# Attention and a gated feed-forward layer on one core: separate places for the inputs of the first four jobs, and mean durations in the planner

## The chip, the cores and the metric

The kernel runs on one core of a Trainium2 chip. The metric is the device time of one execution in microseconds (us); lower is better. TensorE is called PE, VectorE DVE, ScalarE ACT, GpSimd POOL; SP is the engine whose queue issues all DMA transfers here.

## The reference

```python
def _attn_ref(q, k, v, f):                      # (8, 8, 576, 64) each, f (8, 8, 576), all f32
    scores = scale * np.matmul(q, k.transpose(0, 1, 3, 2))
    cum = np.cumsum(np.log(np.clip(f, 0.0001, 1.0)), axis=-1)
    decay = cum[:, :, :, None] - cum[:, :, None, :]
    scores = np.where(causal, -1000000000.0, scores + decay)
    scores = scores - np.max(scores, axis=-1, keepdims=True)
    attn = np.exp(scores)
    attn = attn / (np.sum(attn, axis=-1, keepdims=True) + 1e-09)
    return np.matmul(attn, v)

def _moe_ref(x, w_in, w_out):                   # x (4608, 512), w_in (512, 2048), w_out (2048, 512)
    h = x @ w_in
    g = np.where(h >= 1, h, np.where(h <= -1, 0.0, (h + 1) ** 2 / 4))
    return g @ w_out
```

The attention output of all heads of a token is the feed-forward layer's row x.

## The kernel before

**Work.** Attention runs in 36 jobs of two heads each (`jobs`). The first batch is cut in two: jobs 0 to 3 compute its first 256 rows (two row blocks of 128), jobs 4 to 7 the other 320, and from job 8 on a job is a whole batch (five row blocks, `r`). The feed-forward layer runs in 144 units of 256 tokens by 256 hidden columns (`moe_front` L887, `moe_back` L915), as soon as their tokens are there and their weights are converted. Large products are done as three f16 products of a high and a low part; the first five jobs (`NPE`) use f32 products in the place of that.

**A job.** `load` issues its q and k (L581, L585) into one of two buffers `qk32`; `load_decay` issues, one head at a time, a row of cumulative decay copied to all 128 partitions (`ck`, three buffers, L592); `early_prepare` turns q and k with PE (L618) and copies them with ACT (L619). For each row block `scores` multiplies q and k on PE (L712) while POOL makes the decay term (L718) and masks it (L722); `weights` adds both and takes the row minimum on DVE (L801), takes the exponential on ACT (L805) and normalises; in the first jobs PE and ACT turn the result (L732, L743, L754). `early_values` (L774, L781, L782) multiplies by v.

**The decay.** `decay_sums` loads f (L383), clips it (DVE, L384), takes the logarithm (ACT, L387), sums along the row (DVE, L390) and stores the sums to DRAM as `cum_d` (L393); the `ck` rows are read back from there.

**The weights.** 16 blocks of 1 MB are loaded (`weight_load`, L431). Each costs DVE three steps (L441, L444, L447), ACT a square and a scaling (L451, L455), and DVE one step (L460) or POOL two (L457, L458) for the low part. `LOADS` says how many blocks may have been loaded by which job, `CONVERT` how many pairs are converted in which. The first feed-forward units need blocks 0 to 7 and the first batch's value scale (`value_load` L480, `value_max` L486).

**Order.** The code emits all steps, and then `plan` orders them: it keeps a clock for each engine, gives each step a duration from formulas (`Step.cost`), and picks step by step what can begin first. That order is then fixed for every engine, and each works through its own in that order, SP's queue too.

Of the kernel before, what the change touches and what calls it, by code (L numbers as in the profile page):

```python
# [35 lines left out]
EARLY = ((0, 0, 4), (0, 4, 6), (1, 0, 4), (1, 4, 6), (0, 6, 8), (1, 6, 8))  # L36

CONVERT = {1: 1, 2: 1, 3: 2, 5: 1, 6: 1, 9: 1, 10: 2}
LOADS = {0: 3, 1: 6, 2: 8}
AHEAD = 4  # L40

RAW = (2, 4, 6, 8, 10, 12, 14, "early", 10, 12, 14, "next", "early", 14, "early", "early")
# [5 lines left out]
ENGINES = {"PE": "PE", "DVE": "DVE", "Activation": "ACT", "Pool": "POOL", "SP": "SP"}  # L48
WINDOW = 3413.3
RING = 1500  # L50


class Pool:
# [9 lines left out]
class Step:  # L63
# [25 lines left out]
    def cost(self):  # L89
        e, out = self.engine, self.writes[0]  # L90
        n = out[4]
        scalars = sum(1 for r in self.reads if r[4] == 1)
        wide = [r for r in self.reads if r[4] > 1]
        if e == "PE":
            size, wide32 = self.ins.tile_size or (128, 128), self.reads[0][5] == 4
            half = 64 in tuple(size) and not self.ins.is_transpose
            t = n / 2.4 * ((2 if self.ins.is_transpose else 4) if wide32 else 1) * (0.5 if half else 1)
            return max(t + 3, 100 if wide32 else 28)
        if e == "SP":
            if "Transpose" in self.ins.opcode:  # L100
                return max(1250, 1.05 * n)
            return 380 if n > 500 else 520
        if e == "ACT":
            return 150 + (0.82 if wide and wide[0][0][:2] in ("s_", "ph", "po") else 0.93) * n + 100 * min(len(self.reads) - 1 + len(self.writes) - 1, 3)
        if e == "POOL":
            if self.ins.opcode == "TensorTensor":
                return 350 + 1.7 * n
            return 180 + 0.9 * n if "Affine" in self.ins.opcode else 300 + 1.15 * n
        if wide:
            n = max(n, wide[0][4])  # L110
        fast = len(wide) == 1 and self.ins.opcode == "TensorScalarPtr"
        return 150 + 55 * (scalars > 0) + (0.55 if fast else 1.045) * n + (20 if len(self.writes) > 1 else 0)


def clash(a, b):
# [14 lines left out]
def plan(tc, nc, rings):  # L130
# [36 lines left out]
                    last[name] = s.k  # L167
    follow = [[] for _ in steps]
    for s in steps:
        s.time = s.cost()  # L170
        s.open = len(s.after)
        read = {r[0] for r in s.reads}
        for k in s.after:
            o = steps[k]
            follow[k].append(s)
            same = o.engine == s.engine
            if not same or s.engine == "SP" or s.engine != "PE" and any(w[0] in read for w in o.writes):
                s.waits.append(o)
# [14 lines left out]
    for _ in steps:  # L193
        best = None
        for e, cands in ready.items():
            pick = None
            for k, t in cands.items():
                s = steps[k]
                for name in s.tiles:
                    if name in at:  # L200
                        continue
                    base = name.rsplit("_", 1)[0]
                    j = place[name] - rings[base]
                    if taken[base] != place[name] or j >= 0 and queue[base][j] not in gone:
                        break
                    if j >= 0:
                        t = max(t, gone[queue[base][j]])
                else:
                    c = (max(t, free[e]), k)
                    if pick is None or c < pick:  # L210
                        pick = c
            if pick and (best is None or pick < best[:2]):
                best = pick + (e,)
        t, k, e = best
        s = steps[k]
        del ready[e][k]
# [60 lines left out]
def kernel(  # L277
# [99 lines left out]
    cum_d = dram.tile([B * H, S], F32, name="cum_d")  # L377
    cq = const.tile([P, NT5, B * H], F32, name="cq")

    def decay_sums():  # L380
        fl = early
        nb = B * H
        nc.sync.dma_start(fl[0:nb, 0:S], f.rearrange("b h s -> (b h) s"))  # L383
# [85 lines left out]

    vmax = {}  # L470
    vpart = [None]

    def value_load(b, i):

        if b:
            vpart[0] = one.tile([P, S], F32, name="vst")
        else:
            vpart[0] = stage[:, i * S:(i + 1) * S]
        part = v[b, 2 * i:2 * i + 2].rearrange("h s d -> (h s d)").rearrange("(p n) -> p n", p=P)
        nc.sync.dma_start(vpart[0], part)  # L480

    def value_max(b, i):

        if b not in vmax:
            vmax[b] = tiny.tile([P, NPAIR], F32, name="m4", bufs=2)
        nc.vector.tensor_reduce(  # L486
            out=vmax[b][:, i:i + 1], in_=vpart[0], axis=AX.X, op=ALU.max, apply_absolute_value=True
        )

    def value_step(b, i):  # L490
# [58 lines left out]
    v32 = const.tile([P, 2, NT5, D], F32, name="v32")  # L549
    sdr = [const.tile([P, FULL], F32, name=f"sdr_{i}") for i in range(4)]  # L550
    sd4 = [const.tile([P, SP], F32, name=f"sd4_{i}") for i in range(2)]
    for t in qk32 + [v32]:
        nc.gpsimd.memset(t, 0.0)
    for t in sd4:
        nc.gpsimd.memset(t[:, S:SP], 0.0)

# [3 lines left out]
    def load(ji):  # L560
# [3 lines left out]
        w.sds = {}  # L564
        w.s0, w.s1 = P * w.r0, min(P * w.r1, S)
        w.cuts = [(w.s0, w.s1)] if w.s1 - w.s0 <= 512 else [(0, 64), (64, S)]
        h0 = 2 * w.hp
        flat = qk32[ji % 2].rearrange("p j h t d -> p (j h t d)")
        w.x32 = []
        for j, src in enumerate((q, k)):  # L570
            s_ = src[w.b, h0:h0 + 2]
            t0 = 0 if j else w.r0
# [13 lines left out]
        w.ck = []  # L586
        return w

    def load_decay(w, h):
        bh = w.b * H + 2 * w.hp + h  # L590
# [14 lines left out]
    def early_prepare(w):  # L605
# [6 lines left out]
        for j in range(2):  # L612
            pt = ps.tile([P, 1024], F32, name="s")
            t0 = 0 if j else w.r0
            n = w.s1 - P * t0
            for c0 in range(0, n, P):
# [22 lines left out]
    def prepare(w):  # L639
# [14 lines left out]
        qh, ql, kh, kl = (qkT[:, c] for c in range(4))  # L654
        w.terms = ((qh, kh), (ql, kh), (qh, kl))

    def split_values(w):
        h0 = 2 * w.hp
        s_ = v[w.b, h0:h0 + 2]
        if w.p < NPE:  # L660
# [304 lines left out]
    def weight_step():  # L965
# [6 lines left out]
        for first, end in groups:  # L972
            if nw == 2 * end:
                z = moe_scales(0, first, end - 1, True)
                for ch, e0, e1 in EARLY:
                    if (e0, e1) == (first, end):
                        for fb in range(first, end):
                            bsc[(ch, fb)] = z

    pairs = [load(0)]  # L980
    decay_sums()
    pairs.append(load(1))
    load_decay(pairs[0], 0)
    load_decay(pairs[0], 1)
    prepare(pairs[0])
    for i in range(NPAIR + 1):
        value_step(0, i)
    value_scale(0)
    split_values(pairs[0])
    pairs.append(load(2))  # L990
    for p in range(njobs + 1):
        w = pairs[p] if p < njobs else None
        nxt = pairs[p + 1] if p + 1 < njobs else None
# [1 line left out]
        if w:  # L995
# [7 lines left out]
            def step(r):  # L1003
# [3 lines left out]
                    load_decay(nxt, 1)  # L1007
                    split_values(nxt)
                weights(w, r)
                if r == w.r0 and p + 3 < njobs:  # L1010
# [74 lines left out]
```

## Time and profile before

| | us |
|---|---|
| median of 3 runs | 1097.97 (1097.82 to 1099.86) |
| profiled execution, its own time | 1102.53 |
| its span in the trace | 1100.7 |
| PE busy in the span | 1014.0 (92%) |
| DVE, ACT, POOL busy | 794.6, 795.5, 430.9 |

The profiled execution is 4.56 us above the median and 1.83 us above its own span. Busy times of different engines overlap; an engine can be idle only because it waits for another, and the section of rows shows where.

### The profile page before, as it was taken

Reading aid. Unit: us, or ns where it says so; the run is one execution under the profiler, and the core shown is the slowest. Engines: PE = TensorE matmul, PEld = TensorE weight load, DVE = VectorE, ACT = ScalarE, POOL = GpSimd, SP = SyncE. Lnnn points to the kernel's source line nnn. Section 1 sums busy time; section 2 is a strip of 40 time slices with the busy share of each in tenths; the row PEclk is TensorE's granted clock in tenths of the full one; section 3 lists DMA queues with packets and bytes.
Section 4 is the critical chain, followed back from the end, with each engine's and each line's share of the span. In section 5 each row is a group of like instructions: output and inputs, shape, how many; then the busy total and the mean of one; then the engine's idle time right before and its main releaser. Section 6 shows DMA issues by size and latency. Waiting matters only on the chain.

```text
span 1100.7 us, 24411 instructions
## 1 busy us (share of the span) xinstructions
PE 1014.0 (92%) x8811; PEld 661.4 (60%) x8811; DVE 794.6 (72%) x2095; ACT 795.5 (72%) x1638; POOL 430.9 (39%) x679
## 2 busy tenths in 40 slices
PE   2648988869989999999999999999999999999998
PEld 1435554435666667566666666666666666676665
DVE  6767988899978885987667768877887886322222
ACT  3577887877977886888767878888888877344443
POOL 2484865554543531574223424444445351000000
PEclk9858988988998999999999999999999999999999
DMA  8967677777886885766642656666676653200000
GB/s 262 292 166 236 142 172 163 174 177 170 192 184 165 171 184 103 173 164 135 135 96 72 152 135 159 141 157 146 151 148 148 138 111 85 51 21 1 20 20 20
DMA packets 408281, 152.18 MB, mean 138 GB/s; under 512 B 383968, under 2 KB 384992, under 8 KB 408160
## 3 DMA queue, kind: packets, MB, share of 16 engines
q1 hardware_dynamic: 408160, 150.63, 58.4%
q8 instruction: 69, 1.13, 0.4%
q14 instruction: 52, 0.43, 0.1%
HBM read 75.64 MB, written 9.58 MB: 77 GB/s over the span
## 4 chain that ended last, share of the span: by engine, by line
PE 51%; ACT 3%; DVE 2%; DMA 1%; issue 1%; POOL 0%; DVEq 0%; ACTq 0%; SPq 0%
PE ph L887 23%; PE po L915 22%; PE s L712 4%; PE s L845 3%; DMA qkT<-qs 1%; ACT pr L819 1%; ACT sdr L805 0%; ACT u L896 0%; DMA v<-in_v_dram 0%; ACT u L897 0%; ACT g L900 0%; DVE qs L646 0%; DVE pr L825 0%; DVE u L898 0%; DVE sdr L801 0%
## 5 line engine op out<-in xcount | busy, mean ns | idle before, releaser
L887 PE MATMUL ph<-x,place 128*128 128x256 f16 (+3 forms) x4608 | 421.2, 250 | 9.7 <-DVE u L898 6.9
L915 PE MATMUL po<-place,g 128*128 128x512 f16 x1728 | 402.0, 380 | 1.4 <-DVE g L901 0.9
L887 PEld LDWEIGHTS <-place 128*128 128x128 f16 x4608 | 355.8, 99 | 73.3 <-issue 29.1
L915 PEld LDWEIGHTS <-g 128*128 128x128 f16 x1728 | 165.9, 98 | 176.4 <-issue 6.3
L718 POOL TENSOR_SCALAR sdr<-ck,nsig,cqs 128x128 f32<-128x128 f32 (+1 forms) x192 | 146.6, 770 | 213.9 <-DVE pr L825 188.1
L898 DVE SCALAR_TENSOR_TENSOR u<-ph,z,u 128x512 f32<-128x512 f32 x128 | 95.8, 748 | 121.7 <-ACT u L897 121.1
L805 ACT ACTIVATE sdr<-sdr,nm 128x384 f32<-128x384 f32 (+1 forms) x248 | 137.6, 556 | 46.3 <-DVE nm L801 44.3
L896 ACT ACTIVATE u<-ph,z 128x512 f32<-128x512 f32 x128 | 98.3, 768 | 84.0 <-PE ph L887 83.9
L825 DVE SCALAR_TENSOR_TENSOR pr<-sdr,rc,pr 128x384 f16<-128x384 f32 (+2 forms) x232 | 131.7, 600 | 14.6 <-ACT pr L819 12.0
L900 ACT ACTIVATE g<-u,z 128x512 f16<-128x512 f32 x128 | 92.0, 718 | 67.3 <-DVE u L898 66.9
L712 PE MATMUL s<-qkT 64*64 64x512 f16 (+11 forms) x1056 | 117.6, 342 | 17.4 <-DVE nm L801 10.9
L819 ACT ACTIVATE pr<-sdr,rc 128x384 f16<-128x384 f32 (+1 forms) x236 | 120.5, 556 | 11.7 <-ACT sdr L805 5.0
L718 POOL TENSOR_SCALAR sd<-ck,nsig,cqs 64x576 f32<-64x576 f32 x48 | 56.4, 1174 | 180.2 <-issue 81.4
L901 DVE SCALAR_TENSOR_TENSOR g<-u,z,g 128x512 f16<-128x512 f32 x128 | 97.3, 760 | 32.4 <-ACT g L900 32.2
L801 DVE CUSTOM_DVE_ANT_0 sdr<-s,sdr,nalpha 128x128 f32<-128x128 f32 (+1 forms) x192 | 99.5, 544 | 14.6 <-POOL sdr L722 7.4
L722 POOL TENSOR_SCALAR_AFFINE_SELECT sdr<-sdr 128x128 f32<-128x128 f32 x248 | 95.1, 401 | 5.4
L897 ACT ACTIVATE u<-u 128x512 f32<-128x512 f32 x144 | 89.9, 624 | 2.6
L845 PE MATMUL s<-pT,vs 128*64 128x320 f16 (+3 forms) x1098 | 70.7, 283 | 3.2 <-DVE nm L801 3.2
L718 POOL TENSOR_SCALAR sdr<-ck,cq 128x384 f32<-128x384 f32 (+3 forms) x56 | 44.7, 799 | 58.7 <-DVE pr L825 29.4
L845 PEld LDWEIGHTS <-vs 128*64 128x64 f16 x1098 | 49.0, 112 | 27.6 <-issue 9.2
L712 PEld LDWEIGHTS <-qkT 64*128 64x128 f16 (+1 forms) x864 | 32.8, 98 | 49.6 <-issue 35.1
L644 ACT ACTIVATE qs<-qk,sc 128x640 f16<-128x640 f32 x48 | 37.3, 820 | 17.9 <-DVE sc L370 17.9
(154 smaller groups left out, 1017.0 us busy)
## 6 DMA issues: line engine op xcount, KB each, us to landing
ck<-cum_d SPq DMA_DIRECT2D x64, 288.0 KB, 3.9
out_dram<-ot SPq DMA_DIRECT2D x36, 256.0 KB, 2.0
qk<-in_k_dram SPq DMA_DIRECT2D x64, 128.0 KB, 2.8
vst<-in_v_dram SPq DMA_DIRECT2D x28, 288.0 KB, 3.1
v<-in_v_dram SPq DMA_DIRECT2D x62, 128.0 KB, 2.8
qk<-in_q_dram SPq DMA_DIRECT2D x56, 128.0 KB, 2.7
place<-in_moe_w_in_dram SPq DMA_DIRECT2D x6, 1024.0 KB, 8.2
place<-in_moe_w_out_dram SPq DMA_DIRECT2D x5, 1024.0 KB, 6.7
```

The lines of the kernel that those rows point to most:

```text
L712: nc.tensor.matmul(sds[h % len(sds)][1][p0:p1, c0:c1], lhsT=a[rows, q0 - w.s0:q0 - w.s0 + p1 - p0], rhs=b[rows, c0:c1], start=(i == 0), st ...
L718: nc.gpsimd.tensor_scalar(out=sd[p0:p1, 0:wid], in0=w.ck[h][p0:p1, 0:wid], scalar1=w.nsig if w.p < NQK else w.nsig[p0:p1], scalar2=w.cqs[p ...
L801: nc.vector.tensor_tensor_reduce(out=a, in0=sp[:, 0:wid], in1=a, scale=w.nalpha, scalar=BIG, op0=ALU.add, op1=ALU.min, accum_out=nm[:, i:i ...
L805: nc.scalar.activation(a, a, AF.Exp, bias=nm[:, i:i + 1], scale=-1.0, accum_out=sm[:, i:i + 1])
L819: nc.scalar.activation(pr[:, :, 0, i, :], a, AF.Copy, scale=rc[:, i:i + 1])
L825: nc.vector.scalar_tensor_tensor(out=pr[:, :, 1, i, :], in0=a, scalar=rc[:, i:i + 1], in1=pr[:, :, 0, i, :], op0=ALU.mult, op1=ALU.subtract,)
L845: nc.tensor.matmul(av[64 * h:64 * h + 64, at + s0:at + s1], lhsT=w.vs[:, vl, h, t, :], rhs=w.pT[:, t, pl, h, s0:s1], start=(t == 0 and pi ...
L887: nc.tensor.matmul(ph[:, fi, a0:a1], lhsT=wi[fb][:, wl, t, fi * P:(fi + 1) * P], rhs=xs[b][:, t, xl, s0:s0 + a1 - a0], start=(fi == 0 and ...
L896: nc.scalar.activation(u, h, AF.Relu, scale=z.u[:, i:i + 1], bias=z.h[:, i:i + 1])
L898: nc.vector.scalar_tensor_tensor(out=u, in0=h, scalar=z.t[:, i:i + 1], in1=u, op0=ALU.max, op1=ALU.min)
L901: nc.vector.scalar_tensor_tensor(out=g[:, 1], in0=u, scalar=z.r[:, i:i + 1], in1=g[:, 0], op0=ALU.mult, op1=ALU.subtract)
L915: nc.tensor.matmul(po[ch][i], lhsT=g[:, gl, fi * TC + i * P:fi * TC + (i + 1) * P], rhs=wo[fb][:, wl, fi, :], start=(first and fi == 0 and ...
```

## The change

Jobs 0 to 3 get a place of their own for q and k (two in each `qk32` buffer), for v (two in each `vs` buffer), and for the decay rows (one of the four `ot` buffers each, both heads in one transfer). Their q and k come with one transfer for both heads, and a partition then holds two neighbouring rows of a head (512 B in one piece, where it was two pieces of 256 B); PE turns them with four f32 products against the identity, of 64 columns each, in the place of two transposes of 128. All inputs of these jobs are issued ahead of the job loop, with weight blocks between them. The two large clearings of `qk32` fall away. The planner gets longer durations on DVE, POOL and SP, a factor of 1.03 on all engines but PE, and a rule that among steps which can begin within 50 ns of the engine's being free the one emitted first is taken.

```diff
-LOADS = {0: 3, 1: 6, 2: 8}
+LOADS = {0: 6, 1: 7, 2: 8}
...
+SLOW = 1.03
+LOOK = 50
...
             if "Transpose" in self.ins.opcode:
-                return max(1250, 1.05 * n)
-            return 380 if n > 500 else 520
+                return max(1340, 1.17 * n)
+            return 430 if n > 500 else 620
...
-                return 350 + 1.7 * n
-            return 180 + 0.9 * n if "Affine" in self.ins.opcode else 300 + 1.15 * n
+                return 450 + 2.0 * n
+            return 260 + 0.95 * n if "Affine" in self.ins.opcode else 460 + 1.15 * n
...
-        s.time = s.cost()
+        s.time = s.cost() * (SLOW if s.engine != "PE" else 1)
...
-                    c = (max(t, free[e]), k)
+                    begin = max(t, free[e])
+                    c = (free[e] if begin <= free[e] + LOOK else begin, k, begin)
...
-    for t in qk32 + [v32]:
-        nc.gpsimd.memset(t, 0.0)
+    nc.gpsimd.memset(v32, 0.0)
...
+        if ji < NPAIR:
+            n = 2 * 2 * D
+            for j, src in enumerate((q, k)):
+                at = (2 * (ji // 2) + j) * n
+                w.x32.append(flat[:, at:at + n])
+                nc.sync.dma_start(
+                    w.x32[j].rearrange("p (h e) -> p h e", h=2),
+                    src[w.b, h0:h0 + 2, 0:w.s1].rearrange("h (p n) d -> p h (n d)", p=P),
+                )
+            return w
...
+    def load_first_decay(w):
+        bh = w.b * H + 2 * w.hp
+        ck = two.tile([P, DM], F32, name="ot", bufs=4)
+        ck = ck.rearrange("p (h s) -> p h s", h=2)
+        nc.sync.dma_start(
+            ck, cum_d[bh:bh + 2, 0:w.s1].rearrange("(o h) s -> o h s", o=1).broadcast_to([P, 2, w.s1])
+        )
+        w.ck += [ck[:, 0], ck[:, 1]]
...
+                for i in range(2):
+                    for h in range(2):
+                        nc.tensor.matmul(
+                            cols[64 * h:64 * h + 64, i], lhsT=rows[:, h, i], rhs=ident, start=True, stop=True
+                        )
...
+    decay_load()
     pairs = [load(0)]
+    value_load(0, 0)
+    value_load(0, 1)
+    pairs.append(load(1))
+    value_load(0, 2)
+    value_load(0, 3)
+    first_values(pairs[0])
     decay_sums()
-    pairs.append(load(1))
-    load_decay(pairs[0], 0)
-    load_decay(pairs[0], 1)
+    load_first_decay(pairs[0])
+    load_first_decay(pairs[1])
+    first_values(pairs[1])
+    load_weights(2)
+    for i in range(2, NPAIR):
+        pairs.append(load(i))
+        load_first_decay(pairs[i])
+        first_values(pairs[i])
+        load_weights(2 * i)
     prepare(pairs[0])
```

**What moves, first place.** SP's queue around the store of the decay sums (`cum_d<-x`), before; `place<-in_moe_w_...` are weight blocks, `qk_0` and `qk_1` the two buffers of q and k.

```order
L431 DMA place<-in_moe_w_out_dram 128x2x1024
L431 DMA place<-in_moe_w_in_dram 128x4x512
L393 DMA cum_d<-x 64x576
L670 DMA vs<-in_v_dram 128x2x64 x2
L581 DMA qk_0_98<-in_q_dram 128x2x64 x2
L581 DMA qk_0_98<-in_k_dram 128x2x64 x2
L581 DMA qk_1_99<-in_q_dram 128x2x64 x2
L581 DMA qk_1_99<-in_k_dram 128x2x64 x2
L592 DMA ck<-cum_d 128x256 x3
```

The same place in the changed kernel (L399 is the store, L610 the read of the decay rows of both heads, L583 q and k of both heads).

```order
L701 DMA vs<-in_v_dram 128x2x64 x4
L399 DMA cum_d<-x 64x576
L437 DMA place<-in_moe_w_in_dram 128x4x512
L437 DMA place<-in_moe_w_out_dram 128x2x1024
L583 DMA qk_0_98<-in_q_dram 128x2x128
L583 DMA qk_0_98<-in_k_dram 128x2x128
L610 DMA ot<-cum_d 128x2x256 x3
```

The store now stands ahead of all weight blocks, where it stood behind three, and four transfers stand between it and the first read of the decay rows, where there were ten.

**Second place.** DVE at the program's start, before; `x<-x 64x576` are the steps of the decay (clip, sum), `m` the value maxima.

```order
L384 TENSOR_SCALAR x<-x 64x576
L486 TENSOR_REDUCE m_154<-x 128x1 x4
L499 TENSOR_REDUCE m_162<-m_154 128x1
L352 TENSOR_REDUCE top<-ph 1x1
L353 TENSOR_SCALAR top<-top 1x1
L355 COPY mv<-ph 128x1
L390 SCALAR_TENSOR_TENSOR x<-x 64x576
```

The same in the changed kernel.

```order
L390 TENSOR_SCALAR x<-x 64x576
L494 TENSOR_REDUCE m_179<-x 128x1 x2
L396 SCALAR_TENSOR_TENSOR x<-x 64x576
L402 COPY x<-x 64x128
L494 TENSOR_REDUCE m_179<-x 128x1 x2
```

The sum along the row (the second `x<-x 64x576`) moved ahead of two of the four value maxima and of the steps that join them.

**Third place.** DVE among the scores of job 1 (L801, whose second head's are `pr2_114` and `pr3_115`) and the weight steps (`qs_93`, `place_90`), before.

```order
L444 SCALAR_TENSOR_TENSOR qs_93<-place_90,qs_93 128x1024
L782 SCALAR_TENSOR_TENSOR x_79<-po0_337,sv_96,x_79 128x256
L447 SCALAR_TENSOR_TENSOR place_90<-place_90,qs_93 128x1024
L441 TENSOR_SCALAR qs_93<-place_90 128x1024
L801 ISA pr2_114,nm_299<-s_268,pr2_114 128x128
L801 ISA nm_299 128x1
L801 ISA pr3_115,nm_320<-s_282,pr3_115 128x256
```

The same scores in the changed kernel (L851, the second head's first being `pr2_112`).

```order
L851 ISA pr2_112,nm_299<-s_275,pr2_112 128x128
L851 ISA nm_299 128x1
L447 TENSOR_SCALAR qs_93<-place_90 128x1024
L851 ISA pr3_113,nm_320<-s_287,pr3_113 128x256
L851 ISA nm_320 128x1
L858 TENSOR_SCALAR rc_305<-sm2_300 128x2
```

In the order before, the second head's scores stand behind six weight blocks and the first step of a seventh; now they stand behind three blocks, with the first step of the fourth between them.

## Rows read from the trace of the kernel before

**Rows 1.** The page: the span.

```profile
span 1100.7 us, 24411 instructions
```

**Rows 2.** Busy us by stretch: PE, PEld, DVE, ACT, POOL; clock, DMA share, GB/s.

```profile
25.70:85.00 59.30, 33.01 (x152) 21.62 (x152) 43.20 (x114) 39.00 (x94) 39.38 (x53) 0.70 0.78 235
85.00:110.00 25.00, 20.45 (x127) 14.01 (x124) 18.52 (x44) 19.24 (x44) 12.85 (x18) 0.84 0.79 233
110.00:200.00 90.00, 77.73 (x546) 47.42 (x545) 78.40 (x196) 72.76 (x146) 59.39 (x78) 0.90 0.73 160
200.00:300.00 100.00, 85.56 (x696) 50.52 (x694) 91.62 (x287) 79.60 (x176) 52.31 (x79) 0.91 0.79 178
300.00:400.00 100.00, 95.90 (x901) 63.11 (x900) 84.53 (x239) 79.20 (x171) 43.23 (x74) 0.97 0.81 175
400.00:1100.00 700.00, 695.23 (x6382) 461.36 (x6379) 461.82 (x1195) 498.57 (x1001) 217.48 (x361) 1.00 0.48 109
```

**Rows 3.** Timeline, DVE: the start, and job 0's first scores.

```profile
3.51 1.69 DVE L384 TENSOR_SCALAR x<-x 64x576 f32<-64x576 f32 x1 [3.51 <-DMA x<-in_f_dram]
5.12 2.97 DVE L486 TENSOR_REDUCE m<-x 128x1 f32<-128x576 f32 x4
...
10.05 1.35 DVE L390 TENSOR_TENSOR_SCAN x<-x 64x576 f32<-64x576 f32 x1
...
25.70 0.29 DVE L801 CUSTOM_DVE_ANT_0 sdr<-s,sdr 128x128 f32<-128x128 f32 x1 [2.70 <-POOL sdr L722]
```

**Rows 4.** Timeline, SP's queue around the decay sums and their reads.

```profile
12.31 0.49 SPq L393 DMA_DIRECT2D cum_d<-x  x1
...
15.21 1.63 SPq L581 DMA_DIRECT2D qk<-in_k_dram  x2
19.18 0.88 SPq L581 DMA_DIRECT2D qk<-in_q_dram  x2
...
21.12 1.41 SPq L592 DMA_DIRECT2D ck<-cum_d  x3
```

**Rows 5.** DMA issues from 0 to 20 us: count, KB each, us to landing.

```profile
x<-in_v_dram SPq DMA_DIRECT2D x4, 288.0 KB, 3.8
...
x<-in_f_dram SPq DMA_DIRECT2D x1, 144.0 KB, 2.7
cum_d<-x SPq DMA_DIRECT2D x1, 144.0 KB, 7.2
```

**Rows 6.** Timeline, POOL: decay terms of jobs 0, 1 and 2.

```profile
24.38 0.38 POOL L718 TENSOR_SCALAR sdr<-ck,cq 128x128 f32<-128x128 f32 x1 [18.60 <-DMA ck<-cum_d]
...
28.80 0.54 POOL L722 TENSOR_SCALAR_AFFINE_SELECT pr<-pr 128x128 f32<-128x128 f32 x2
38.28 2.62 POOL L718 TENSOR_SCALAR pr<-ck,cq 128x128 f32<-128x128 f32 x2 [8.94 <-DMA ck<-cum_d]
...
43.75 1.47 POOL L722 TENSOR_SCALAR_AFFINE_SELECT sdr<-sdr 128x128 f32<-128x128 f32 x2
```

**Rows 7.** Busy time by stretch: POOL's wait for ck, and the 8 us after.

```profile
29.33:38.28 8.95, 6.28 (x30) 4.52 (x30) 8.72 (x19) 5.20 (x16) 0.01 (x1) 1.00 1.07 370
38.28:46.40 8.12, 3.73 (x16) 2.52 (x17) 7.01 (x18) 3.02 (x11) 7.48 (x10) 0.58 1.04 335
```

**Rows 8.** DVE's groups from 25.7 to 85 us: busy, mean ns, idle before.

```profile
L444 DVE SCALAR_TENSOR_TENSOR qs<-place,qs 128x1024 int32<-128x1024 int32 x4 | 4.9, 1221 | 0.0
L447 DVE SCALAR_TENSOR_TENSOR place<-place,qs 128x1024 int32<-128x1024 int32 x4 | 4.9, 1220 | 0.0
...
L441 DVE TENSOR_SCALAR qs<-place 128x1024 int32<-128x1024 int32 x4 | 2.9, 734 | 2.3 <-DMA place<-in_moe_w_out_dram 2.2
L486 DVE TENSOR_REDUCE m<-vst 128x1 f32<-128x576 f32 x4 | 2.9, 733 | 0.0
```

**Rows 9.** Timeline, DVE and PE: job 4's last 512-wide score, and the first unit.

```profile
84.40 0.68 DVE L801 CUSTOM_DVE_ANT_0 sdr<-s,sdr 128x512 f32<-128x512 f32 x1
...
96.51 0.61 PE L887 MATMUL ph<-x,place 128*128 128x256 f16 x4
```

More of the change, by code (lines that the diff above doesn't have):

```diff
@@ L111, in cost @@
         fast = len(wide) == 1 and self.ins.opcode == "TensorScalarPtr"
-        return 150 + 55 * (scalars > 0) + (0.55 if fast else 1.045) * n + (20 if len(self.writes) > 1 else 0)
+        return 170 + 55 * (scalars > 0) + (0.6 if fast else 1.08) * n + (20 if len(self.writes) > 1 else 0)
 def clash(a, b):
@@ L208, in plan @@
                 else:
-                    c = (max(t, free[e]), k)
+                    begin = max(t, free[e])
+                    c = (free[e] if begin <= free[e] + LOOK else begin, k, begin)
                     if pick is None or c < pick:
                         pick = c
-            if pick and (best is None or pick < best[:2]):
-                best = pick + (e,)
+            if pick and (best is None or (pick[2], pick[1]) < best[:2]):
+                best = (pick[2], pick[1], e)
         t, k, e = best
@@ L378, with decay_load @@
     cq = const.tile([P, NT5, B * H], F32, name="cq")
+    def decay_load():
+        nc.sync.dma_start(early[0:B * H, 0:S], f.rearrange("b h s -> (b h) s"))
     def decay_sums():
@@ L382, in decay_sums @@
         nb = B * H
-        nc.sync.dma_start(fl[0:nb, 0:S], f.rearrange("b h s -> (b h) s"))
         nc.vector.tensor_scalar(
@@ L471 @@
     vpart = [None]
+    vparts = []
     def value_load(b, i):
@@ L478, in value_load @@
             vpart[0] = stage[:, i * S:(i + 1) * S]
+            vparts.append(vpart[0])
         part = v[b, 2 * i:2 * i + 2].rearrange("h s d -> (h s d)").rearrange("(p n) -> p n", p=P)
@@ L486, in value_max @@
         nc.vector.tensor_reduce(
-            out=vmax[b][:, i:i + 1], in_=vpart[0], axis=AX.X, op=ALU.max, apply_absolute_value=True
+            out=vmax[b][:, i:i + 1], in_=vpart[0] if b else vparts[i], axis=AX.X, op=ALU.max, apply_absolute_value=True
         )
@@ L566, in load @@
         w.cuts = [(w.s0, w.s1)] if w.s1 - w.s0 <= 512 else [(0, 64), (64, S)]
+        w.ck = []
         h0 = 2 * w.hp
@@ L585, in load @@
                 nc.sync.dma_start(dst[0:64, :, nt - 1, :], s_[:, FULL:S, :].rearrange("h p d -> p h d"))
-        w.ck = []
         return w
+    def load_first_decay(w):
[6 more added lines that the diff above has]
+        w.ck += [ck[:, 0], ck[:, 1]]
     def load_decay(w, h):
+        if w.p < NPAIR:
+            return
         bh = w.b * H + 2 * w.hp + h
@@ L615, in early_prepare @@
             n = w.s1 - P * t0
-            for c0 in range(0, n, P):
+            if w.p < NPAIR:
+                rows = w.x32[j].rearrange("p (h n d) -> p h n d", h=2, n=2)
+                cols = pt[:, 0:n].rearrange("c (p n) -> c n p", n=2)
+                for i in range(2):
[3 more added lines that the diff above has]
+                        )
+            for c0 in range(0, n if w.p >= NPAIR else 0, P):
                 m = min(P, n - c0)
@@ L655, in prepare, with first_values @@
         w.terms = ((qh, kh), (ql, kh), (qh, kl))
+    def first_values(w):
+        h0 = 2 * w.hp
+        if w.p % 2 == 0:
+            t = two.tile([P, 2, 2, NT5, D], F16, name="vs")
+            pairs_v[0] = t.rearrange("p l h t d -> p (l h t d)").bitcast(F32)
+        n = 2 * 2 * D
+        w.vs = pairs_v[0][:, (w.p % 2) * n:(w.p % 2 + 1) * n].rearrange("p (h t d) -> p h t d", h=2, t=2)
+        for hh in range(2):
+            nc.sync.dma_start(w.vs[:, hh], v[w.b, h0 + hh, 0:w.s1, :].rearrange("(t p) d -> p t d", p=P))
+    pairs_v = [None]
     def split_values(w):
+        if w.p < NPAIR:
+            return
         h0 = 2 * w.hp
@@ L978, in weight_step @@
                             bsc[(ch, fb)] = z
+    decay_load()
     pairs = [load(0)]
-    decay_sums()
-    pairs.append(load(1))
-    load_decay(pairs[0], 0)
-    load_decay(pairs[0], 1)
+    value_load(0, 0)
[4 more added lines that the diff above has]
+    first_values(pairs[0])
+    decay_sums()
+    load_first_decay(pairs[0])
[7 more added lines that the diff above has]
+        load_weights(2 * i)
     prepare(pairs[0])
-    for i in range(NPAIR + 1):
-        value_step(0, i)
+    for i in range(NPAIR):
+        value_max(0, i)
     value_scale(0)
-    split_values(pairs[0])
-    pairs.append(load(2))
     for p in range(njobs + 1):
@@ L1009, in step @@
                 weights(w, r)
-                if r == w.r0 and p + 3 < njobs:
+                if r == w.r0 and NPAIR <= p + 3 < njobs:
                     pairs.append(load(p + 3))
```

## Prediction

> **What bounds the kernel now.** The span is 1100.7 us [rows 1]. I read the table by stretch first, PE's column: from 400 us to the end PE is busy 695.23 of 700 us at full clock, so there PE is the bound and little is to be had. Ahead of that it is not: it lacks 4.6 us of 25 from 85 on, 12.3 of 90, 14.4 of 100 and 4.1 of 100, 35.4 us in all up to 400, while DVE is busy 91.62 of 100 between 200 and 300 [rows 2]. From 25.7 to 85 us PE has 33 busy us of 59.3, and at a granted clock of 0.70. So the end of the kernel is the point from which PE is full plus a fixed amount of PE work, and a microsecond taken out of the beginning comes off the end, unless the stretch from 85 to 400 us takes it back.
>
> So I read the beginning closely. The first scores of job 0 reach DVE at 25.70 us [rows 3]. Behind them stands a chain: f lands (3.51), DVE clips, four value maxima stand ahead of the sum (10.05 to 11.4), the store is issued at 12.31 and lands 7.2 us later, the read of the decay rows is issued at 21.12 because SP's queue stood still from 16.84 to 19.18 with four more transfers ahead of it, and POOL begins at 24.38 [rows 3 to 6].
>
> Then POOL has done half of job 1 by 29.3 us and waits 8.94 us for the next decay row, up to 38.28 [rows 6]: there were three `ck` buffers. What the reader should see is that DVE did not stand still meanwhile: it was busy 8.72 of these 8.95 us [rows 7], with weight steps. The wait is therefore no direct loss; it made the weights run ahead of attention, and DVE and ACT waited for each other and for POOL later. From 25.7 to 85.0 us, where job 4's last 512-wide score pass stands [rows 9], DVE was busy 43.20, ACT 39.00 and POOL 39.38 of 59.3 us [rows 2]: three engines of about equal load, each idle for a third of the time.
>
> **The change, part by part.**
>
> *The start.* The value transfers stand behind f, q and k now. f's issue is at 0.75 and takes 0.60; with two more at 0.49 like the store's [rows 4] the first two values are issued at about 2.35 and 2.85, and land by 6.65 at 3.8 us each [rows 5]. Two maxima at 2.97/4 = 0.74 end at 7.4, the sum's 1.35 at 8.75 [rows 3], and the store goes out at 8.9, 3.4 us sooner. It had two weight blocks ahead of it and has none now. Its landing lies between 2.7 us (f, of the same 144 KB) and the old 7.2 [rows 5]; I take 3.0, near f, since what was issued ahead of it is small by then. The reads go out at 11.9. Ahead of them in the DMA queues are two weight blocks, issued at 9.4 and 9.9. By the old case, where the store went out 0.6 us after its second block and landed 7.2 later, these are through by 9.9 + 0.6 + 7.2 = 17.7; 0.5 MB more (q, k and the row itself) at 370 GB/s [rows 7] are 1.4 us. That is 17.7 to 19.1 for POOL's start; the store at its old price gives 16.1 + 3.3 = 19.4. I take 18.5 in place of 24.38. Job 0's score on DVE came 1.32 us after POOL's start, so 19.8; but two weight blocks stand ahead of it on DVE, each 0.73 + 1.22 + 1.22 = 3.17 us [rows 8], and if the second lands at 17.7 they end at 20.9. I take 20.3: **5.4 us sooner** (4.8 to 6.3).
>
> *From there to job 4's score (25.7 to 85.0 before).* DVE has three blocks done ahead of job 0's score before and two now, so one more falls in this stretch: +3.17. The four maxima of the next batch's values, 2.9 us there [rows 8], stand later in the new order: -2.9. DVE's work is then 43.5 us. If nothing ever waited the stretch would be 43.5 us, a gain of 15.8; if the engines wait for each other as before, 59.6, a loss of 0.3. The decay wait is gone, each of the four jobs finds its inputs, and the scores are spread between the weight steps, so ACT, which was busy 5.20 of 8.95 us during the wait and 3.02 of 8.12 after it [rows 7], gets its exponentials while the squares are still few. Against that, what DVE did alone now meets POOL's work: two masks took 0.54 us at 28.80 and 1.47 at 43.75, when DVE was busy 7.01 of 8.12 us [rows 6, 7]. Jobs 1 to 3 have 24 POOL steps, 10 of which lie in that loaded stretch already; seven more pairs at up to 0.93 are 6.5 us more on POOL, which has 19.9 idle. I take half of DVE's 16.1 idle us as regained, and 2 us of it as lost again to POOL: **6 us**.
>
> *What I cost at nothing.* The clearing of `qk32` ran on POOL long before 24.38, where POOL waited. The four f32 products per q or k instead of two transposes are some microsecond a job on PE, which is idle 26 of 59.3 us there; if PE were full this would cost 4 us in all. Transfers of both heads halve the issues on SP's queue; the queue counts only through the start, above. Per-step planner costs change no duration, only order.
>
> *After 85 us.* The new order has, ahead of the values of nearly every job, the same number of feed-forward units as the old to within about one, and the same weight blocks converted. So I take the rest as shifted whole, with the deferred maxima falling where DVE has room (461.82 of 700 us from 400 on [rows 2]). What the new order does to the 35.4 us that PE lacks there I cannot read from the old trace; I allow a tenth of it either way, 4 us.
>
> *Sum.* 5.4 + 6 = 11.4, rounded to 11. The profiled execution took 1102.53 us, so 1091.5 in its terms; it lies 4.56 above the median of the runs, so the median goes from 1097.97 to **1087**. With the bounds of both terms and the 4 us after them, 1080 to 1094.
>
> **The rivals.**
>
> *Only the start is gained.* If the three engines wait for each other as much as before, the 6 us are not there: 1092.6. For it: the waits in this stretch are spread over many pairs, and the decay wait itself cost DVE 0.2 us. Against it: the order there is another.
>
> *All of the idle time is regained.* 5.4 + 15.8 = 21: 1077. It needs three engines at over 90% with a chain between them; only DVE from 200 to 300 us comes near that [rows 2].
>
> *The gain is taken back before PE is full.* DVE is the engine nearest its limit from 110 to 400 us. If the re-planned stretch loses 11 us of DVE or PE there, or if the second eight weight blocks bind in place of the first, the time stays at 1098. Nothing in the rows shows such a fixed point; but the change re-plans the whole kernel, so it is possible.
>
> *Slower: POOL and DVE hold each other up.* The scores now run among the weight steps, and rows show POOL's steps stretched to nearly three times beside them. There are 64.7 us from 20.3 to the old 85.0 and DVE needs 43.5 of them, so it decides once more than 21.2 us of DVE's time is lost to POOL's 39 to 46 us of work. At 30 us lost the score falls at 93.8, 8.8 later than before: 1107. The Trainium skill speaks for this case: its page "SBUF — State Buffer", section "SBUF: two separate sides", says that DVE, in some modes or with two SBUF inputs, and GpSimd take a shared port pair for a whole instruction, the other one blocking fully. By that rule taken at its hardest, every POOL step here would come off DVE's time. The trace agrees with stretched POOL steps (0.54 against 1.47), but not with that hardest form, since both were busy over 7 us of the same 8.12 [rows 7].
>
> **How the numbers follow.** Forecast 0.57 (1080 to 1091), only the start 0.19 (1091 to 1094), all regained 0.06, taken back 0.10, slower 0.08. Some 0.2%, 2.2 us, is what a measurement of this kernel can tell. Faster: 0.57 + 0.19 + 0.06 = 0.82; same 0.10; slower 0.08. The range from 1078 to 1098 leaves out the slower case, most of the full regain and part of the taken-back one, a little under 2 in 10.
>
> **What would show it.** In the changed trace the store should be issued near 8.9 us and POOL should begin at 18 to 19.5; job 0's first score on DVE near 20.3; no wait for a decay row over a microsecond or two in jobs 1 to 3; job 4's last 512-wide score ending near 73.6 instead of 85.0, the first unit near 85 instead of 96.5; PE's idle time up to 400 us shorter by about 11, and 400 to the end as full as before. The forecast is wrong if the score of job 4 comes sooner but PE's idle time from 85 to 400 grows (taken back), or if POOL's steps fill its time without a gap up to job 4 (slower), or if weight blocks land later than DVE asks for them.

## The result, and the profile after

The changed kernel takes 1081.99 us (median of 4 runs, 1077.43 to 1083.67), the kernel before 1097.89 beside it; the ratio is 0.9846 (95% interval 0.9812 to 0.9881). Forecast were 1087, a range from 1078 to 1098, and "faster" at 0.82. The gain is 15.9 us, not 11.

The two profiled executions lie further apart than the medians: 1102.53 us before (above all four runs beside it) and 1077.43 after (the fastest of its four), 25.1 us. A second profile of the changed kernel, of 1084.76 us, stands below as e4 and guards against reading the difference of two single executions as the change's.

The table by stretch of the changed kernel, with columns as in [rows 2] (22.74 to 78.71 us is its stretch from job 0's first score to job 4's last 512-wide one):

```profile
0.00:100.00 100.00, 62.95 (x340) 39.88 (x341) 76.66 (x174) 63.39 (x145) 61.38 (x89) 0.75 0.81 250
22.74:78.71 55.97, 38.02 (x181) 23.60 (x182) 47.42 (x116) 41.69 (x100) 42.79 (x51) 0.62 0.74 227
...
100.00:200.00 100.00, 88.58 (x606) 51.35 (x606) 90.84 (x225) 81.85 (x169) 69.51 (x89) 0.96 0.74 169
200.00:300.00 100.00, 90.07 (x842) 56.60 (x837) 95.64 (x297) 83.46 (x180) 53.75 (x79) 0.93 0.83 178
300.00:400.00 100.00, 99.73 (x989) 65.68 (x987) 86.50 (x245) 83.85 (x182) 42.55 (x76) 1.00 0.88 185
400.00:1075.00 675.00, 671.09 (x6091) 443.05 (x6089) 442.77 (x1158) 478.93 (x964) 205.17 (x346) 1.00 0.49 110
```

From 400 us on PE is as full as before. The reader should look at 200 to 400: PE is full, at full clock, from 300 us on, where it had 95.90 busy us of 100 at 0.97, and between 200 and 300 it has 90.07 where it had 85.56. The forecast let this stretch be shifted and no more.

The milestones, from the timelines of SP, POOL, DVE and PE of the changed kernel (L399 is the store of the decay sums, L610 the reads, L768 POOL's decay term, L851 the score pass, L937 a unit's first matmuls); they answer to [rows 3, 4, 6, 9]:

```profile
9.12 0.48 SPq L399 DMA_DIRECT2D cum_d<-x  x1
...
12.18 2.82 SPq L610 DMA_DIRECT2D ot<-cum_d  x3
...
20.40 1.94 POOL L768 TENSOR_SCALAR sdr<-ot,cq 128x128 f32<-128x128 f32 x2 [17.34 <-DMA ot<-cum_d]
...
22.74 0.29 DVE L851 CUSTOM_DVE_ANT_0 sdr<-s,sdr 128x128 f32<-128x128 f32 x1 [0.63 <-POOL sdr L772]
...
78.03 0.68 DVE L851 CUSTOM_DVE_ANT_0 sdr<-s,sdr 128x512 f32<-128x512 f32 x1
...
88.19 1.27 PE L937 MATMUL ph<-x,place 128*128 128x256 f16 x10
```

And DMA issues of the changed kernel from 0 to 22 us (count, KB each, us to landing), which answer to [rows 5]:

```profile
x<-in_v_dram SPq DMA_DIRECT2D x4, 288.0 KB, 4.4
ot<-cum_d SPq DMA_DIRECT2D x4, 256.0 KB, 8.2
...
cum_d<-x SPq DMA_DIRECT2D x1, 144.0 KB, 2.3
```

The store left and landed nearly as worked out, the reads took 8.2 us behind two weight blocks, and POOL's first two steps took 1.94 us in place of two of 0.38. So job 0's first score came 3.0 us sooner, not 5.4; job 4's last 512-wide pass ended at 78.71 instead of 85.08, 6.4 sooner, not 11.4; the first unit came 8.3 sooner.

To see where the rest came from, I read off each timeline when DVE writes the low part of a job's x (in the kernel before L782 up to job 4 and L855 from job 5 on), and subtract. The lead over the kernel before, in us, at some of the 36 jobs (the column "before" is its own time):

```
job                before   changed  e4 again  e1 inputs  e2 planner  e5 maxima  e11 DVE/ACT
3                   85.09       6.5       7.0        8.3         0.2       -1.6          0.2
4                  106.41       7.5       5.4       10.6         1.8       -1.3          5.8
8                  196.91      14.6      10.0       13.9         4.9        2.1          7.2
12                 300.83      13.9       7.5       13.0         4.9        3.1          8.4
13                 329.01      18.4      12.2       11.7        14.1        6.2         14.1
14                 358.28      23.4      17.4       11.9        14.0        8.7         17.5
20                 529.34      24.0      16.7        9.8        15.9        8.9         18.6
```

After job 20 no column moves by over 2 us. The changed kernel has 7 us at job 3 and gains ten more between jobs 12 and 14, in both of its profiles. Between jobs 3 and 12 the two profiles of this one kernel part by some 6 us (13.9 and 7.5 at job 12), so a lead read off one execution is good to no better than that. The inputs alone bring 8 to 11 by job 4 and nothing after job 8; the planner alone has almost nothing at job 4 and 14 at job 13.

### The profile page after: what moved, and what is told of

The parts are those of the page before. It is cut to its first block, busy times and chain, and to the rows that moved or that the text cites. A ratio compares the mean times of both kernels' runs of the same rounds, so it can differ in the third digit from the quotient of the medians.

```text
span 1075.7 us, 24444 instructions
## 1 busy us (share of the span) xinstructions
PE 1012.4 (94%) x8859; PEld 656.6 (61%) x8859; DVE 792.4 (74%) x2095; ACT 791.5 (74%) x1638; POOL 432.4 (40%) x677
## 4 chain that ended last, share of the span: by engine, by line
PE 65%; DVE 1%; ACT 1%; DMA 1%; issue 1%; SPq 0%; POOL 0%; POOLq 0%; DVEq 0%
PE ph L937 29%; PE po L965 27%; PE s L762 5%; PE s L895 4%; DMA vst<-in_v_dram 0%; DMA ck<-cum_d 0%; DVE pr L875 0%; DVE sdr L851 0%; ACT sdr L855 0%; POOL sdr L768 0%; PE ph L365 0%; ACT pr L869 0%; ACT g L950 0%; POOL sd L768 0%; SPq L603 0%
## 5 line engine op out<-in xcount | busy, mean ns | idle before, releaser
L937 PE MATMUL ph<-x,place 128*128 128x256 f16 (+3 forms) x4608 | 414.6, 247 | 3.2 <-ACT x L904 2.2
L937 PEld LDWEIGHTS <-place 128*128 128x128 f16 x4608 | 352.1, 98 | 65.6 <-issue 25.2
L768 POOL TENSOR_SCALAR sdr<-ck,nsig,cqs 128x128 f32<-128x128 f32 (+1 forms) x192 | 154.0, 808 | 242.8 <-DVE pr L875 231.6
L855 ACT ACTIVATE sdr<-sdr,nm 128x384 f32<-128x384 f32 (+1 forms) x248 | 137.3, 555 | 23.2 <-DVE nm L851 20.9
L875 DVE SCALAR_TENSOR_TENSOR pr<-sdr,rc,pr 128x384 f16<-128x384 f32 (+2 forms) x232 | 127.6, 583 | 17.4 <-ACT pr L869 15.8
L762 PE MATMUL s<-qkT 64*64 64x512 f16 (+11 forms) x1056 | 122.3, 341 | 8.4 <-DVE x L905 3.5
L851 DVE CUSTOM_DVE_ANT_0 sdr<-s,sdr,nalpha 128x128 f32<-128x128 f32 (+1 forms) x192 | 100.0, 543 | 17.4 <-PE s L762 11.7
L768 POOL TENSOR_SCALAR sd<-ck,nsig,cqs 64x576 f32<-64x576 f32 x48 | 48.0, 1000 | 137.8 <-issue 57.3
L772 POOL TENSOR_SCALAR_AFFINE_SELECT sdr<-sdr 128x128 f32<-128x128 f32 x248 | 97.6, 410 | 5.3
L768 POOL TENSOR_SCALAR sdr<-ck,cq 128x384 f32<-128x384 f32 (+3 forms) x48 | 41.1, 857 | 34.8 <-DVE pr L875 24.3
L682 DVE SCALAR_TENSOR_TENSOR qs<-qk,sc,qs 128x640 f16<-128x640 f32 x48 | 44.6, 943 | 4.2 <-ACT qs L680 4.2
```

Of the source, the lines that this page charges most:

```text
L762: nc.tensor.matmul(sds[h % len(sds)][1][p0:p1, c0:c1], lhsT=a[rows, q0 - w.s0:q0 - w.s0 + p1 - p0], rhs=b[rows, c0:c1], start=(i == 0), st ...
L768: nc.gpsimd.tensor_scalar(out=sd[p0:p1, 0:wid], in0=w.ck[h][p0:p1, 0:wid], scalar1=w.nsig if w.p < NQK else w.nsig[p0:p1], scalar2=w.cqs[p ...
L772: nc.gpsimd.affine_select(sd[p0:p1, q0:wid], sd[p0:p1, q0:wid], pattern=[[-1, wid - q0]], channel_multiplier=1, base=0, compare_op=ALU.is_ ...
L851: nc.vector.tensor_tensor_reduce(out=a, in0=sp[:, 0:wid], in1=a, scale=w.nalpha, scalar=BIG, op0=ALU.add, op1=ALU.min, accum_out=nm[:, i:i ...
L855: nc.scalar.activation(a, a, AF.Exp, bias=nm[:, i:i + 1], scale=-1.0, accum_out=sm[:, i:i + 1])
L875: nc.vector.scalar_tensor_tensor(out=pr[:, :, 1, i, :], in0=a, scalar=rc[:, i:i + 1], in1=pr[:, :, 0, i, :], op0=ALU.mult, op1=ALU.subtract,)
```

## The experiments

Each is compared with the kernel before on the same chip.

**e1 and e2: the change in two halves.** e1 has the changed inputs and the planner as it was; e2 the old inputs and the whole new planner.

```diff
 # e1: changed kernel with
-SLOW = 1.03
-LOOK = 50
 # and the old Step.cost and choice of step; e2: kernel before with the new ones
```

e1, expected: 

> The changed inputs with the planner as it was. Theory A (the inputs bring the gain at the start, and the rest of the kernel is shifted whole): POOL's first decay term near 20.4 us, job 4's values 6 to 8 us sooner than before, and about 1088 to 1092 us. Theory B (most of the gain comes later, from the new order): the same start, but a lead that does not grow after job 4, and 1090 to 1094. If the inputs alone give the whole gain, 1080 to 1084.

Measured: 1090.35 us, ratio 0.9896 (0.9857 to 0.9935).

e2, expected: 

> The inputs as before with the new planner (durations, factor, rule of 50 ns). Theory A: no gain beyond 4 us, 1094 to 1100. Theory B: the lead grows between jobs 12 and 15, as it does in the changed kernel, and the time is 1084 to 1092 although the start is as before.

Measured: 1088.92 us, ratio 0.9905 (0.9874 to 0.9937).

Each half alone is worth about 1%. The product of the two ratios, 0.980, lies just outside the interval of the result (0.9812 to 0.9881) and inside that of e4 (0.9796 to 0.9851). e1 alone does not part the theories, since 1090.35 lies in both ranges: POOL begins at 19.73, job 4's values come 10.6 us sooner (theory A asked for 6 to 8), and the lead is then carried. e2 does part them: its time lies in theory B's range and outside A's, with a lead that comes between jobs 12 and 13. So A's account fits the inputs, B's the planner, and neither alone holds for the whole change.

PE's idle time says where e1 gains. Its first 100 us and the 300 us after them, first of the kernel before and then of e1 (columns as above):

```profile
0.00:100.00 100.00, 54.02 (x259) 35.80 (x260) 68.31 (x165) 56.53 (x132) 51.60 (x83) 0.80 0.81 250
100.00:400.00 300.00, 264.80 (x2176) 164.23 (x2175) 264.51 (x737) 240.37 (x507) 161.80 (x236) 0.93 0.77 170
0.00:100.00 100.00, 64.06 (x373) 44.57 (x373) 81.66 (x187) 65.61 (x149) 66.85 (x93) 0.77 0.84 256
100.00:400.00 300.00, 266.26 (x2264) 166.33 (x2265) 260.36 (x736) 240.97 (x512) 156.80 (x234) 0.93 0.79 175
```

PE idles 46.0 us of the first 100 before and 35.9 in e1, 10.0 less, and the span of e1 is 10.3 us shorter (1090.4). From 100 to 400 us it idles 35.2 and 33.7, at the same granted clock of 0.93: the inputs do not repair the middle. The changed kernel idles 37.1 and, by its rows in the result, 21.6.

**e3: the decay rows alone.** The first four jobs' decay rows in the `ot` buffers, both heads in one transfer; all else, the planner too, as before.

```diff
+    def load_first_decay(w):
+        ck = two.tile([P, DM], F32, name="ot", bufs=4)
...
     def load_decay(w, h):
+        if w.p < NPAIR:
+            if h == 0:
+                load_first_decay(w)
+            return
```

> The kernel before with one thing changed: the decay rows of jobs 0 to 3 in the output buffers, both heads in one transfer, so that POOL no longer waits 8.9 us in job 1. Theory A (that wait cost nothing by itself, DVE having had weight steps to do): within 3 us of before, 1095 to 1100. Rival (the wait sat on the path): 8 us less, near 1090.

Measured: 1090.91 us, ratio 0.9921 (0.9895 to 0.9947). The time is the rival's, but the place is not. POOL's wait is gone; its timeline, in the stretch where it stood still before:

```profile
31.32 2.51 POOL L735 TENSOR_SCALAR_AFFINE_SELECT pr<-pr 128x128 f32<-128x128 f32 x2
33.93 0.84 POOL L731 TENSOR_SCALAR sdr<-ot,cq 128x128 f32<-128x128 f32 x2
34.83 2.07 POOL L735 TENSOR_SCALAR_AFFINE_SELECT sdr<-sdr 128x128 f32<-128x128 f32 x2
```

Yet the lead is only 3.5 us at job 3 and 3.0 at job 4; it is 16.4 at job 9 and ends near 12. Every change of inputs makes the planner order everything anew, so this run changed more than the wait. Hence the next.

**e9: the decay rows apart, the order kept.** The planner is shown these rows under the old buffer's name, with three places, so that each engine's order is that of before.

```diff
+            if h == 0:
+                w.rows = two.tile([P, DM], F32, name="ot", bufs=4)
+            ck = w.rows[:, h * w.s1:(h + 1) * w.s1]
...
+        return (f"ck_own{2 * own.index(part[0]) + h}", *part[1:3], ...
```

> The kernel before in its own order on every engine, with its own transfers; only the places of the decay rows of jobs 0 to 3 are separate, so that no read of one waits for a buffer. Theory A (the 8.9 us wait is no direct loss; what decay_only gained came from its other order): within 3 us of before. Rival (the wait is the loss): 5 to 9 us less.

Measured: 1099.87 us, ratio 1.0005 (0.9992 to 1.0018). The number is theory A's, but the run did not do what it was made for: the wait is still there. SP's queue and POOL in its timelines:

```profile
27.13 3.24 SPq L609 DMA_DIRECT2D ot<-cum_d  x2
...
38.84 2.92 POOL L739 TENSOR_SCALAR pr<-ot,cq 128x128 f32<-128x128 f32 x2 [7.80 <-DMA ot<-cum_d]
```

The wait is 7.80 us with a buffer for each row, where it was 8.94, and POOL goes on no sooner (38.84, where it was 38.28). In this order what held the row was its place in the queue, behind the weight blocks issued from 23.42 to 26.39, and not a full buffer. In e3 the row came with one of the first three reads, ahead of all these blocks:

```profile
20.95 1.49 SPq L593 DMA_DIRECT2D ot<-cum_d  x3
22.49 0.47 SPq L431 DMA_DIRECT2D place<-in_moe_w_out_dram  x1
```

There one transfer brings both heads, and the planner, which counts buffers, sees four in the place of three; which of the two moved the read forward was not tested. What the wait by itself costs e9 cannot say; e11 below says something of it.

**e5: the value maxima without their wait.** In the middle, something had to explain job 13. In the kernel before DVE and PE show this in their timelines:

```profile
321.42 0.75 DVE L486 TENSOR_REDUCE m<-vst 128x1 f32<-128x576 f32 x1 [3.79 <-DMA vst<-in_v_dram]
322.14 2.85 PE L887 MATMUL ph<-x,place 128*128 128x64 f16 x48
...
330.77 5.28 PE L887 MATMUL ph<-x,place 128*128 128x64 f16 x48 [3.08 <-DVE u L898]
```

Its stretch from 330 us, and its waits for value rows between 85 and 420 us (us in total, times, longest):

```profile
330.00:340.00 10.00, 9.22 (x76) 6.72 (x75) 6.74 (x18) 5.31 (x8) 2.08 (x5) 0.67 0.85 178
```

```profile
DVE m L486 <- DMA vst<-in_v_dram: 8.9, 6, 3.8
```

A value maximum of the next batch stands in DVE's order ahead of work that PE needs, and waits 3.79 us for a row that came late. PE then waits 3.08 us, the granted clock between 330 and 340 us is 0.67 (part of that stretch at the lower of its two levels, 1.2 GHz), and 48 matmuls that took 2.85 us at 322.14 take 5.28, 2.43 more. Gap and slower matmuls make 5.5 us. It is not one execution's accident: e9, in the same order, has it too, with 4.63 us of DVE's wait, a gap of PE of 3.85 and the same 5.28:

```profile
318.57 0.75 DVE L500 TENSOR_REDUCE m<-vst 128x1 f32<-128x576 f32 x1 [4.63 <-DMA vst<-in_v_dram]
...
327.91 5.28 PE L908 MATMUL ph<-x,place 128*128 128x64 f16 x48 [3.85 <-DVE u L919]
```

e5 keeps order and loads, but lets the maxima of later batches read a constant.

```diff
+            s.reads = [row]
...
+        if b:
+            nc.vector.tensor_reduce(
+                out=vmax[b][:, i:i + 1], in_=ones.unsqueeze(1).broadcast_to([P, 4, P]), axis=AX.XY, op=ALU.max,
...
+            return
```

> The kernel before in its own order, but the value maxima of batches 1 to 7 read a constant row of ones in place of the loaded row (the loads are still made, nothing waits for them; the scale so comes from 1.0 and not from the largest value, and the output is the same up to rounding). Theory C (these maxima, waiting for late value rows, hold DVE and with it PE between 85 and 400 us; the new durations put them later): 4 to 10 us less than before, and the lead at job 13 jumps as in the changed kernel. Rival (the wait is covered): within 2 us of before.

Measured: 1094.1 us, ratio 0.9937 (0.9919 to 0.9956), 6.7 us less than its neighbours before. The same place in e5, by stretch:

```profile
320.00:330.00 10.00, 10.00 (x115) 7.06 (x113) 9.16 (x20) 7.57 (x12) 7.58 (x11) 1.00 0.94 190
330.00:340.00 10.00, 9.91 (x80) 6.07 (x73) 9.89 (x45) 8.28 (x23) 4.01 (x8) 1.00 0.78 172
```

PE is full there and its clock 1.00. Theory C holds for this place: e5's lead rises by 5.6 us between jobs 12 and 14 (table), near the 5.5 worked out above, for one wait of one small instruction queued ahead of others. The 6.7 us are the price of all these waits together.

**e6, e7, e8, e10, e11: the planner in parts**, each on the kernel before: SP's durations; the rule of 50 ns; all durations without the rule; POOL's durations with their 1.03; DVE's and ACT's with theirs.

```diff
 # e6
-                return max(1250, 1.05 * n)
-            return 380 if n > 500 else 520
+                return max(1340, 1.17 * n)
+            return 430 if n > 500 else 620
 # e7
+LOOK = 50
...
+                    c = (free[e] if begin <= free[e] + LOOK else begin, k, begin)
 # e8: all durations and SLOW, without the lines of e7
 # e10
-                return 350 + 1.7 * n
-            return 180 + 0.9 * n if "Affine" in self.ins.opcode else 300 + 1.15 * n
+                return 450 + 2.0 * n
+            return 260 + 0.95 * n if "Affine" in self.ins.opcode else 460 + 1.15 * n
...
+        s.time = s.cost() * (1.03 if s.engine == "POOL" else 1)
 # e11
-        return 150 + 55 * (scalars > 0) + (0.55 if fast else 1.045) * n + ...
+        return 170 + 55 * (scalars > 0) + (0.6 if fast else 1.08) * n + ...
...
+        s.time = s.cost() * (1.03 if s.engine in ("DVE", "ACT") else 1)
```

e6: 

> The kernel before with only the planner's durations of SP's queue changed (430 and 620 ns an issue in place of 380 and 520, transposes 1340 or 1.17 ns an element). Theory C: value rows are then expected later, their maxima placed later, waits for them under 5 us in 85 to 420, and 5 to 10 us less. Rival (other durations or the 50 ns rule bring it): within 3 us of before.

Measured 1096.45, ratio 0.9959 (0.9933 to 0.9985): a small gain, 4.4 us, just under the 5 that theory C asked and over the 3 of its rival.

e7: 

> The kernel before with only the rule of 50 ns in the planner. Theory C: little, within 4 us of before, since durations stay. Rival (the rule keeps the emitted order and that is what helps): 8 to 11 us less, like the whole new planner with the old inputs.

Measured 1098.64, ratio 0.9981 (0.9966 to 0.9995): 2 us, within theory C's 4.

e8: 

> The kernel before with all new durations and the factor of 1.03, without the rule of 50 ns. Theory C: 8 to 11 us less, like the whole new planner, with the lead growing between jobs 12 and 15. Rival (the rule): within 3 us of before.

Measured 1084.25, ratio 0.9854 (0.983 to 0.9877): more than the whole new planner on the same inputs.

e10: 

> The kernel before with only POOL's durations in the planner longer (and the 1.03 on POOL). Theory D (POOL's steps, which DVE stretches to two or three times, were the most underestimated, so this part brings most of the 16 us of all durations): 1086 to 1092. Rival (no one part; each brings some): 1094 to 1099.

Measured 1099.45, ratio 0.999 (0.9976 to 1.0003): nothing. Theory D falls.

e11: 

> The kernel before with only DVE's and ACT's durations in the planner longer (and the 1.03 on both). Theory D: within 4 us of before. Rival (DVE is the engine that binds there, so its durations matter most): 1086 to 1092.

Measured 1083.02, ratio 0.985 (0.9824 to 0.9876): all of it, and below the 1086 to 1092 of the rival. A few small numbers in the planner, the constants of DVE's formula 3 to 13% longer and 3% on DVE and ACT, bring as much on the old inputs as the whole change does. Its stretches, and one row of its table of waits between 26 and 50 us (us in total, times, longest):

```profile
0.00:100.00 100.00, 56.73 (x287) 38.02 (x287) 72.82 (x173) 62.25 (x142) 57.32 (x87) 0.85 0.78 244
100.00:400.00 300.00, 274.88 (x2371) 173.20 (x2372) 269.50 (x757) 249.59 (x525) 166.49 (x247) 0.95 0.81 177
...
300.00:400.00 100.00, 100.00 (x991) 65.95 (x989) 87.65 (x256) 85.84 (x182) 48.72 (x80) 1.00 0.84 181
```

```profile
POOL pr L718 <- DMA ck<-cum_d: 8.8, 1, 8.8
```

The decay wait of job 1 is in this kernel at full length, 8.8 us, and the kernel is 17 us faster than before. That wait therefore is not what has to go for such a gain. PE's idle time tells the mirror image of e1: 43.3 us of the first 100 (46.0 before), and 25.1 from 100 to 400 us (35.2 before), with a higher granted clock in both (0.85 for 0.80, 0.95 for 0.93). From 300 us on PE lacks nothing.

Theory C does not account for this. e11 still has 8.0 us of waits for value rows between 85 and 420 us and gains everything; e10 has 3.7 and gains nothing. These waits explain the place at 330 us in the order of before, not what the durations bring in general. On the old inputs the three planners with DVE's and ACT's new durations (e2, e8, e11) gain 0.9 to 1.5%, the three without them (e6, e7, e10) at most 0.4%; e3, without them too but with another order, gained 0.8%.

**e4 and e12: the changed kernel again, and without the rule.**

e4: 

> The changed kernel once more, for a second profile and a narrower interval: 1078 to 1085 us. If the growth of the lead at jobs 13 to 15 (from 14 to 24 us in the first profile) belongs to the order, this profile shows it again; if it belongs to that one execution, the lead stays near 14.

Measured 1078.48 (median of 6), ratio 0.9823 (0.9796 to 0.9851). The growth of the lead at jobs 12 to 14 is there again, so it belongs to the order.

```diff
 # e12: changed kernel with
-                    begin = max(t, free[e])
-                    c = (free[e] if begin <= free[e] + LOOK else begin, k, begin)
+                    c = (max(t, free[e]), k)
```

e12: 

> The changed kernel without the rule of 50 ns. On the old inputs the durations without the rule gave 1084 and with it 1089. If that is the rule's own price, this is 3 to 5 us below the changed kernel, 1074 to 1078, and beats both; if it is chance of one order, it lies within 3 us of the changed kernel.

Measured 1077.7 us, ratio 0.9796 (0.9775 to 0.9816). Its median is the lowest of all kernels here, but its interval overlaps that of e4, so the rule's price on the new inputs is not shown; on the old inputs the intervals of e2 and e8 (0.9874 to 0.9937 and 0.983 to 0.9877) barely touch. With the durations alone at 0.9854 (e8) and inputs besides at 0.9796, the inputs add some 0.6% on top of them, where alone they bring 1.0%: the shares of the two halves depend on each other.

## Why the prediction was right, and where it was mis-sized

**The end as the sum of the beginning.** That PE is full from 400 us on, and that time taken out ahead of it comes off the end, held in every run: after job 20 leads move by 2 us at most.

**The start, 5.4 us: measured 3.0.** Scan, store (9.12 for 8.9) and its landing (2.3 for 3.0) were nearly right; by the sum's own numbers the first value row lands at 6.15, so that two maxima of 0.74 end at 7.6 and not at 7.4, and that is the store's 0.2 us. The reads landed 8.2 us behind two weight blocks, so POOL began at 20.40 and not at 18.5, and its first two decay steps took 1.94 us beside DVE's weight steps instead of 0.76. The 1.32 us from POOL's start to the first score came from a row in which DVE had little to do; here it was 2.34.

**From there to job 4, 6 us: measured 3.4.** (78.71 - 22.74 = 55.97 us in place of 85.08 - 25.70 = 59.38.) Idle time came back as reckoned and more: DVE has 8.6 idle us in this stretch where the sum left it 9.8. What was mis-sized is DVE's own work, 47.42 busy us where the sum had 43.5. The sum charged the meeting of the two engines to POOL alone; the rows show DVE's steps held as well. The rival "slower" has its mechanism here, though not its price. DVE and POOL in the changed kernel's timelines:

```profile
44.00 2.08 DVE L858 TENSOR_SCALAR rc<-sm 128x2 f32<-128x2 f32 x1
...
56.95 3.15 DVE L466 SCALAR_TENSOR_TENSOR place<-place,sw 128x1024 f16<-128x1024 f32 x1
```

```profile
42.97 3.08 POOL L464 TENSOR_TENSOR place<-place 128x1024 f16<-128x1024 f32 x1
...
55.89 3.13 POOL L464 TENSOR_TENSOR place<-place 128x1024 f16<-128x1024 f32 x1
```

A DVE step on two elements a partition, which takes 0.16 us at 60.02, takes 2.08 while POOL's product of 42.97 to 46.05 is running, and the step at 56.95, of a kind that takes 1.30 at 42.78, ends 1.08 us after POOL's at 55.89 has ended. The rule of the Trainium skill's page "SBUF — State Buffer", section "SBUF: two separate sides", that one of the two holds a shared port pair for a whole instruction, agrees with these rows. Other steps ran side by side at their usual lengths:

```profile
38.81 1.05 POOL L768 TENSOR_SCALAR pr<-ot,cq 128x256 f32<-128x256 f32 x2
38.95 0.42 DVE L851 CUSTOM_DVE_ANT_0 sdr<-s,sdr 128x256 f32<-128x256 f32 x1
```

POOL's two terms of this shape took 1.05 us at 23.05 too, while DVE was mostly idle. The prediction took it against the rule's hardest form that both engines were busy over 7 us of the same 8.12. That reading does not carry: a step that is held counts as busy, as the 2.08 us show. Rows like these two do.

**The decay wait.** That the 8.9 us were no direct loss is likely but not shown: e9, made to test it, kept the wait; e11 keeps it and gains 17 us elsewhere; e3 without it leads by only 3 us at job 4, in another order. What the prediction had wrong is why the wait was there. It named the three `ck` buffers; e9 shows the wait with a buffer for each row, so in that order it was the read's place in the queue. What the buffers do through the planner, which counts them when it places the read, was not tested apart.

**After 85 us, 0 within 4 us: measured about 10.** This is the step that failed. The two terms that were worked out brought 3.0 + 3.4 = 6.4 us, which would have given 1091.6; the term put at nothing brought the rest of the 15.9, and that the sum of 11 came as near as it did is luck. The prediction held that the planner's new costs change only the order, and took the new order as worth nothing because the number of units ahead of each job was alike. What differs is finer: which small step stands ahead of which on DVE. It allowed a tenth, either way, of the idle time that PE has ahead of 400 us; from 100 to 400 us the changed kernel takes off more than a third (35.2 to 21.6 us, 23.1 in e4), with a granted clock of 0.96 (0.95) for 0.93. e5 shows one such place and its price; e11 shows that DVE's and ACT's durations in the planner are enough for the whole amount. Which other places make up the rest of e11's 17 us is not settled: none of its waits for value rows stops PE as at 330, and the counts say nothing of the others. How far any new order would have gained by chance is open too; e7 and e10 did not, e6 a little, e3 did.

**The rivals.** "Only the start" (1092.6) is near e1 in time (1090.35) but not in its way: e1 leads by 8.3 us at job 3, so its stretch up to job 4 gained as well. "All regained" did not happen: DVE kept 8.6 idle us and had more work. "Taken back" did not happen either, though the second eight weight blocks bind once in the changed kernel, where DVE waits 3.44 us for one at 85.01.

## What to carry to other kernels

When a planner sets the order, a change of inputs is also a change of order, and the two must be measured apart: here the inputs alone were worth 1.0%, the new durations alone 1.5% and both together 2.0% (e1, e8, e12). Look for small instructions that wait for a transfer ahead of work that the bound engine needs; their price is not their wait but the bound engine's gap and what its clock takes to come back. And before adding buffers for a late transfer, see when it was issued and what was queued ahead of it.

## What was not expected of the hardware

DVE's clip of f took 1.69 us before, while POOL was clearing buffers, and 0.45 in the changed kernel, where the clearing had ended by 3.07 us:

```profile
3.70 0.45 DVE L390 TENSOR_SCALAR x<-x 64x576 f32<-64x576 f32 x1 [3.70 <-DMA x<-in_f_dram]
```

So the clearing, which the prediction put at nothing, went with a DVE step 1.24 us longer, though no run has the one without the other; in the changed kernel the maxima ahead of the sum waited for value rows up to 6.36 us anyway. And the same store of 144 KB landed in 2.3 us with only value rows ahead of it and in 7.2 us behind two weight blocks [rows 5].
